# New order and engines for the second half of batch 0 and for batch 1 of a linear-attention and MLP-mixer kernel

## The chip, the cores and the metric

One core of a Trainium2 chip. The metric is the device time of the kernel in microseconds (us): the median of several executions. Inside the core five engines run their own instruction streams: PE (matrix products), DVE, ACT and POOL (element work), and SP (issues most of the transfers). POOL issues transfers too, on a queue of its own.

## The reference

Four batches, eight heads, 768 steps, 48 values per head and step. A linear attention with a decaying state is followed by a mixer of two perceptrons.

```python
for t in range(S):                       # S = 768
    kt, vt, rt = k[:, :, t], v[:, :, t], r[:, :, t]
    cur = einsum('bhd,bhe->bhde', u * kt, vt)
    y[:, :, t] = einsum('bhd,bhde->bhe', rt, state + cur)
    state = w * state + einsum('bhd,bhe->bhde', kt, vt)
x = y as (batch, 768, 384)
h = relu(xT @ w_tok1) @ w_tok2           # 768 -> 256 -> 768, over the steps
u = x + hT
out = u + relu(u @ w_ch1) @ w_ch2        # 384 -> 1536 -> 384, over the channels
```

## The kernel before

**Tiles.** A batch is cut into six chunks of 128 steps. `unit(b, c)` makes one chunk: scaled copies of k and r (`kr`), their transposes (`trk`, `tr_ps`, copied to `rka`, `rkb`), the scores (`at_ps`, masked to `AT`), the state (`kv_ps`, `S`), the chunk's outputs (`y_ps`) and the product of each step with itself, the own term (`ad_ps`, `adg`, then `ydb` or `yd`), all added to `x_b`. r of two chunks comes in one load, `win` (384 KB); k and v come chunk by chunk (`kt`, `vt`, 192 KB each). In batches 0 and 1 PE transposes; in batches 2 and 3 a transposing transfer does (`rk<-kr`, `uT<-u_sb`).

`mixer(b)` makes the rest of a batch: the hidden layer over the steps (`h_ps<-x_b,wtok`, `h1r`), back to the chunks and transposed (`hx_ps`, copied to `uT`, six pieces in two halves `sg` of three pieces `m`), the up products (`z_ps<-uT,wch`, 12 blocks `jt` for each half, relu to `zr`), the down products (`h_ps<-wch,zr`), the sum `osb` and its store.

**Order.** Each piece of work is a task with a number. A table written out by hand, `ORDER`, lists the numbers in the order in which they are emitted, and each engine keeps that order (`keep_in_program_order`), so that an instruction which waits holds everything behind it on its engine. `ENGINES` chooses the engine of every task that more than one engine can do, in the order in which these tasks are made; `BUFS` gives each tile its buffer. `FILL` puts products of zeros (`warm`) on PE ahead of a task. All are emitted through the same helper, so nearly every instruction has line 281 in the profile.

```python
    def run(self):
        done = set()
        for n in self.order:
            emit, deps = self.tasks[n]
            assert done.issuperset(deps), n
            self.now = n
            emit()
            done.add(n)
```

**Loads.** `load(b, c, i)` issues k, r or v (i = 0, 1, 2) on SP. `HOLD` lets a load of batch 0, and the first two of batch 1, wait until an earlier load has landed, so that four are in flight: r of (1,0) waits for v of (0,3), k of (1,0) for v of (0,4). `GATES` lets later loads wait for a weight: k of (1,2) for weight 2, v of (1,1) for weight 3. The seven weight transfers are issued by POOL between its other work: 0 `wtok1`, 1 `wtok2`, 2 the first four up blocks (`wch_0`), 3 the other eight (`wch_1`, 768 KB), 4 to 6 the thirds of the down weight; `W_DEP` lets some of them wait for a load.

```python
            if (b, c, i) in GATES:
                after(asked[b, c, i], sent[GATES[b, c, i]])
            if (b, c, i) in HOLD:
                after(asked[b, c, i], asked[HOLD[b, c, i]])
```

Of the kernel before, what the change touches and what calls it, by code (L numbers as in the profile page):

```python
# [60 lines left out]
]  # L61
BUFS = {
    'AT0': [
    0, 1, 2, 0, 1, 0, 2, 1, 0, 2, 0, 1, 0, 2, 1, 0, 2, 1, 0, 2, 1, 0, 2, 1,
],
    'AT1': [
    0, 1, 2, 0, 1, 0, 2, 1, 0, 2, 1, 0, 1, 2, 0, 2, 1, 0, 2, 0, 1, 2, 0, 1,
],
    'S0': [
    0, 1, 2, 0, 1, 2,  # L70
# [5 lines left out]
    0, 0, 0, 0,  # L76
],
    'adg': [
    0, 1, 2, 3, 4, 1, 2, 0, 3, 4, 1, 2, 0, 3, 4, 1, 2, 3, 1, 4, 3, 0, 2, 1,
],  # L80
    'h1r': [
    0, 1, 0, 1,
],
    'kp': [
    0, 1, 2, 3, 4, 5, 0, 1, 4, 2, 3, 0, 5, 1, 4, 2, 3, 5, 4, 0, 3, 1, 5, 2, 4, 3, 1, 0, 5, 2,
],
    'kt': [
    0, 1, 2, 3, 4, 5, 0, 1, 2, 3, 4, 5, 0, 1, 2, 3, 4, 0, 5, 1, 2, 3, 0, 4,
],
    'ku': [  # L90
    0, 1, 2, 0, 1, 0, 2, 0, 1, 2, 0, 2,
# [2 lines left out]
    0, 0, 0, 0, 0, 0, 0, 0, 0, 0,  # L94
],
# [8 lines left out]
],  # L104
    'osb': [
    0, 1, 2, 1, 0, 2, 2, 1, 0, 0, 2, 2, 2, 0, 1, 0, 0, 0, 2, 1, 0, 2, 1, 0, 2,
],
    'pr': [
    0, 1, 1, 0, 1, 0, 1, 0, 1, 0, 1, 0,
],  # L110
    'rk': [
    0, 1, 2, 3, 0, 1, 3, 2, 0, 1, 2, 3,
# [8 lines left out]
    0, 1, 0, 1, 0, 1, 1, 0, 0, 1, 0, 1,  # L121
],
    'rt': [
    0, 1, 2, 3, 4, 1, 2, 3, 0, 1, 4, 2,
],
    'uT': [
    0, 1, 2, 3, 0, 1, 2, 3,
# [2 lines left out]
    0, 1, 2, 3, 0,  # L130
],
    'vb': [
    0, 1, 2, 3, 4, 0, 1, 2, 3, 4, 0, 1, 2, 4, 0, 3, 1, 2, 4, 0, 1, 2, 3, 4,
],
    'vt': [
    0, 1, 2, 3, 4, 5, 0, 1, 2, 3, 4, 5, 0, 1, 2, 3, 5, 4, 0, 1, 2, 3, 5, 4,
],
    'win': [
    0, 1, 2, 1, 0, 2,
],  # L140
    'yd': [
    0, 1, 2, 0, 1, 2, 0, 1, 2, 0, 1, 2, 1, 0, 2, 1, 0, 1,
],
    'ydb': [
    0, 1, 0, 0, 1, 0,
],
    'zr': [
    0, 1, 2, 1, 0, 2, 1, 0,
],
}  # L150
ENGINES = [
# [25 lines left out]
WIDE_AT = [  # L177
    0, 1, 2, 3, 4, 5, 6, 7, 8, 9, 10, 11,
]
FILL = {138: 2, 154: 1, 159: 1, 190: 1, 160: 4, 907: 2}  # L180
POOL_ONLY = [
    2, 3,
]
# [59 lines left out]
def kernel(  # L243
# [63 lines left out]
    def fill(bank, fresh):  # L307
        for i in range(FILL.get(plan.now, 0)):
            pe.matmul(bank, warm[:, 0:128], warm[:, 0:bank.shape[-1]], start=fresh, stop=True, skip_group_check=True)
# [246 lines left out]
    def new_bank(tag):  # L556
        bank[0] = psum.tile([128, 512], f32, name="kv_ps", tag=tag, bufs=1)
# [630 lines left out]
    def keep_warm(cols):  # L1188
        def f():
            fresh = bank[0] is None  # L1190
            if fresh:
                new_bank("kv0")
            for i in range(1 + FILL.get(plan.now, 0)):
                pe.matmul(bank[0][:, 512 - cols:512], warm[:, 0:128], warm[:, 0:cols], start=fresh or cols == 512, stop=True,
# [40 lines left out]
```

## Time and profile before

| | |
|---|---|
| runs | 161.89, 162.02, 163.2 us (median 162.02) |
| profiled execution | 162.77 us, of which the span is 161.0 |
| PE busy | 153.7 us (95%) |
| DVE busy | 112.7 us (70%) |
| POOL busy | 88.0 us (55%) |
| ACT busy | 67.5 us (42%) |
| transferred | 26.88 MB, 167 GB/s on average |

The profile covers one execution. An engine is busy while it executes; PE's products are pipelined. A row of the timeline gives start, duration, engine, line and operation, with what is written and read, the shape, and how many are grouped; in brackets the idle time before the row and what ended it. A transfer is issued at its row's start and lands later. Transfers issued by SP run on queue q1, those by POOL on q0.

### The profile page before, as it was taken

The numbers are of one execution on the slowest core, as the hardware profiler recorded it, in microseconds if no ns is written. First come the engines' busy times: TensorE is split into PE (matmuls) and PEld (weight loads), VectorE is DVE, ScalarE is ACT, GpSimd is POOL, SyncE is SP. The second block draws the span as 40 slices with busy tenths as digits, with TensorE's granted clock in tenths as the row PEclk, the third lists the DMA queues.
The fourth block names the chain that finished last, engine by engine and source line by source line (L and its number), as shares of the span: only waits on it lengthen the run. The fifth ranks groups of instructions, "written<-read, shape, count | busy, mean of one in ns | idle before, by whom it ended". The sixth has DMA issues, their size and how long they took to land.

```text
span 161.0 us, 3787 instructions
## 1 busy us (share of the span) xinstructions
PE 153.7 (95%) x1464; PEld 102.3 (64%) x1465; DVE 112.7 (70%) x241; ACT 67.5 (42%) x151; POOL 88.0 (55%) x112
## 2 busy tenths in 40 slices
PE   6998889999999999999899999999999999999992
PEld 1455567767767776666577666677667556666672
DVE  6699889559648996586679946777999555616623
ACT  3998754735642551265357024256441101602100
POOL 7149675007437897999998997699724000000000
PEclk9999999999999999999999999999999999999999
DMA  4999999999999999997999999899991051701133
GB/s 123 221 210 190 147 240 199 145 204 187 212 218 199 175 199 180 253 175 174 183 236 191 203 227 180 162 236 226 140 234 70 0 122 49 219 4 49 49 139 106
DMA packets 93060, 26.88 MB, mean 167 GB/s; under 512 B 87794, under 2 KB 92148, under 8 KB 93044
## 3 DMA queue, kind: packets, MB, share of 16 engines
q1 hardware_dynamic: 90688, 23.40, 74.1%
q0 software_dynamic: 2160, 3.15, 11.7%
q8 instruction: 11, 0.18, 0.5%
q10 hardware_dynamic: 196, 0.11, 0.2%
q14 instruction: 5, 0.04, 0.1%
HBM read 20.46 MB, written 4.72 MB: 156 GB/s over the span
## 4 chain that ended last, share of the span: by engine, by line
PE 55%; DMA 20%; POOL 14%; DVE 4%; issue 3%; ACT 1%; SPq 1%; POOLq 0%; DVEq 0%; ACTq 0%
PE h_ps L281 23%; PE z_ps L281 19%; DMA kt<-in_k_dram 12%; POOL kr L281 8%; DMA rk<-kr 7%; PE y_ps L281 4%; POOL ku L281 3%; PE at_ps L281 3%; PE kv_ps L281 2%; POOL rku L281 2%; PE hx_ps L281 2%; DMA out_dram<-osb 2%; DVE AT L281 1%; POOL yd L281 1%; PE hT_ps L281 1%
## 5 line engine op out<-in xcount | busy, mean ns | idle before, releaser
L281 PE MATMUL h_ps<-wch,zr 128*128 128x384 bf16 (+1 forms) x300 | 54.3, 320 | 0.0
L281 PE MATMUL z_ps<-uT,wch 128*128 128x384 bf16 x288 | 51.8, 326 | 0.0
L281 ACT ACTIVATE zr<-z_ps 128x384 bf16<-128x384 f32 x62 | 28.4, 492 | 42.5 <-PE z_ps L281 42.3
L281 PEld LDWEIGHTS <-wch 128*128 128x128 bf16 x288 | 31.7, 114 | 13.1
L281 PEld LDWEIGHTS <-zr 128*128 128x128 bf16 x300 | 27.2, 98 | 15.4 <-issue 0.2
L281 DVE TENSOR_TENSOR AT<-at_ps,mask 128x512 bf16<-128x512 f32 x48 | 31.1, 684 | 6.5 <-PE at_ps L281 6.2
L281 POOL TENSOR_TENSOR kr<-kt,wnat 128x384 bf16<-128x384 f32 x21 | 20.9, 998 | 18.5 <-DMA kt<-in_k_dram 17.8
L281 DVE TENSOR_SCALAR zr<-z_ps 128x384 bf16<-128x384 f32 x34 | 18.5, 554 | 11.6 <-PE z_ps L281 11.4
L281 POOL TENSOR_TENSOR yd<-vb,adg 128x384 f32<-128x384 bf16 x18 | 14.9, 829 | 6.7 <-ACT vb L281 4.3
L281 PEld LDWEIGHTS <-kr 128*128 128x128 bf16 x176 | 11.2, 99 | 5.0 <-issue 1.0
L281 ACT CAST vb<-vt 128x384 bf16<-128x384 f32 x22 | 10.9, 513 | 8.2 <-DMA vt<-in_v_dram 8.0
L281 DVE TENSOR_TENSOR osb<-u_sb,h_ps 128x384 f32<-128x384 bf16 (+1 forms) x16 | 8.3, 526 | 7.3 <-PE h_ps L281 4.6
L281 POOL TENSOR_TENSOR rku<-ku,rt 128x384 f32<-128x384 f32 x12 | 11.9, 998 | 0.1
L281 POOL TENSOR_TENSOR kr<-rt,wp 128x384 bf16<-128x384 f32 x12 | 11.9, 999 | 0.1
L281 POOL TENSOR_TENSOR ku<-kt,u_bc 128x384 f32<-128x384 f32 x12 | 11.9, 999 | 0.0
L281 DVE TENSOR_TENSOR x_b<-y_ps,yd 128x384 bf16<-128x384 f32 x18 | 9.6, 551 | 1.9 <-PE y_ps L281 1.1
L281 PEld LDWEIGHTS <-wtok 128*128 128x128 bf16 x78 | 7.4, 98 | 4.4
L281 DVE TENSOR_TENSOR u_sb<-x_b,hT_ps 128x384 bf16<-128x384 bf16 x15 | 7.8, 550 | 2.9 <-PE hT_ps L281 2.7
L281 PE MATMUL h_ps<-x_b,wtok 128*128 128x384 bf16 x48 | 8.8, 326 | 0.0
L281 ACT ACTIVATE h1r<-h_ps 128x384 bf16<-128x384 f32 x4 | 2.0, 491 | 16.2 <-PE h_ps L281 16.2
L281 PE MATMUL y_ps<-vb,AT 128*128 128x48 bf16 x192 | 8.8, 183 | 0.0
L281 PEld LDWEIGHTS <-rk 64*128 64x128 bf16 (+1 forms) x136 | 5.3, 95 | 3.4 <-DMA rk<-kr 1.4
(96 smaller groups left out, 182.0 us busy)
## 6 DMA issues: line engine op xcount, KB each, us to landing
kt<-in_k_dram SPq DMA_DIRECT2D x24, 192.0 KB, 4.8
vt<-in_v_dram SPq DMA_DIRECT2D x24, 192.0 KB, 4.1
out_dram<-osb SPq DMA_DIRECT2D x23, 192.0 KB, 2.3
win<-in_r_dram SPq DMA_DIRECT2D x6, 384.0 KB, 6.0
rt<-in_r_dram SPq DMA_DIRECT2D x12, 192.0 KB, 4.1
wch<-in_moe_w_ch_dram POOLq DMA_DIRECT2D x4, 384.0 KB, 6.9
wtok<-in_moe_w_tok_dram POOLq DMA_DIRECT2D x2, 384.0 KB, 6.0
wch<-in_moe_w_ch_dram POOLq DMA_DIRECT2D x1, 768.0 KB, 8.9
```

Source lines behind the costliest of these rows:

```text
L281: return lambda *args, **kw: tc.keep_in_program_order(f(*args, **kw))
```

## The change

Only tables change: `ORDER`, `BUFS`, `ENGINES` and `FILL`. The tasks and what they compute stay. `ORDER` is new from the middle of batch 0 on to about the down products of batch 0's mixer and the last chunk of batch 1, and holds small swaps after that; from the hidden layer of batch 1's mixer on, PE's order is the old one. `HOLD`, `GATES` and `W_DEP` are the old ones. Five products of zeros go (one ahead of the scores of a chunk of batch 0, four ahead of an output), three come in ahead of the state of chunk 2.

```diff
 ORDER = [
...
-    906, 136, 156, 907, 185, 41, 152, 204, 66, 169, 131, 190, 205, 153, 141, 67, 50, 143, 170, 40, 191, 142, 171, 119,
+    906, 136, 156, 907, 185, 152, 66, 169, 131, 153, 174, 50, 67, 170, 137, 141, 176, 190, 142, 204, 40, 175, 69, 167,
...
-    222, 226, 209, 214, 223, 232, 227, 224, 219, 197, 228, 225, 216, 237, 217, 229, 122, 333, 230, 233, 231, 334, 246,
+    215, 209, 224, 228, 214, 196, 232, 227, 219, 122, 197, 225, 216, 229, 217, 333, 237, 230, 233, 231, 334, 240, 234,
...
 ENGINES = [
-    0, 0, 1, 0, 1, 1, 1, 1, 1, 0, 1, 0, 1, 1, 1, 0, 0, 0, 1, 0, 1, 1, 1, 1, 0, 1, 1, 0, 0, 0, 1, 1, 0, 0, 0, 0, 0, 0,
+    0, 0, 1, 0, 1, 1, 1, 1, 1, 0, 1, 0, 1, 1, 1, 0, 0, 1, 1, 0, 1, 1, 1, 1, 0, 1, 1, 0, 0, 0, 1, 1, 0, 1, 0, 0, 0, 0,
...
-FILL = {138: 2, 154: 1, 159: 1, 190: 1, 160: 4, 907: 2}
+FILL = {138: 2, 154: 1, 159: 1, 907: 2, 177: 3}
```

The first place is POOL at the end of batch 0, where it issues the weights: before the change its rows there are these. `ydb` are own terms, `kr_71<-kt` is the key product of the last chunk of batch 0, `wtok_100` and `wtok_101` are the token weights, `wch_0` and `wch_1` the two parts of the up weight; `kr_67<-kt` belongs to chunk 2 of batch 1.

```order
L281 TENSOR_TENSOR wGm_94<-bm,wG_91 128x384
L281 DMA wtok_100<-in_moe_w_tok_dram 128x6x256
L281 TENSOR_TENSOR ydb<-vb,adg 128x384 x2
L281 TENSOR_TENSOR kr_71<-kt,wnat_84 128x8x48
L281 DMA wtok_101<-in_moe_w_tok_dram 128x1536
L281 DMA wch_0_102<-in_moe_w_ch_dram 128x3x512
L281 TENSOR_TENSOR ydb<-vb,adg 128x384 x2
L281 DMA wch_1_103<-in_moe_w_ch_dram 128x3x1024
L281 TENSOR_TENSOR kr_67<-kt,wnat_84 128x8x48
```

And these are they after the change:

```order
L281 TENSOR_TENSOR wGm_94<-bm,wG_91 128x384
L281 DMA wtok_100<-in_moe_w_tok_dram 128x6x256
L281 TENSOR_TENSOR kr_71<-kt,wnat_84 128x8x48
L281 DMA wtok_101<-in_moe_w_tok_dram 128x1536
L281 DMA wch_0_102<-in_moe_w_ch_dram 128x3x512
L281 TENSOR_TENSOR ydb<-vb,adg 128x384 x2
L281 DMA wch_1_103<-in_moe_w_ch_dram 128x3x1024
L281 TENSOR_TENSOR kr_69<-win,wpair 128x8x48
L281 TENSOR_TENSOR kr_67<-kt,wnat_84 128x8x48
```

The two own terms ahead of the last key product are gone from that place (one is done earlier, one on DVE), and with it the second token weight and both parts of the up weight move up. A product of the first window of batch 1 has come over from DVE.

The second place is DVE at the start of batch 0's up products, before the change. `kr_70<-kt` is the key product of chunk 0 of batch 1, `uT` are the pieces that the up products read.

```order
L281 TENSOR_TENSOR kr_69<-win,wpair 128x8x48 x2
L281 TENSOR_SCALAR h1r<-h_ps 128x384
L281 CAST uT<-hx_ps 128x3x128
L281 TENSOR_TENSOR kr_70<-kt,wnat_84 128x8x48
L281 CAST uT<-hx_ps 128x3x128
L281 COPY rka<-trk 128x512
L281 TENSOR_SCALAR zr<-z_ps 128x384 x2
```

After the change DVE has there:

```order
L281 TENSOR_TENSOR kr_69<-win,wpair 128x8x48
L281 TENSOR_SCALAR h1r<-h_ps 128x384
L281 TENSOR_TENSOR kr_70<-kt,wnat_84 128x8x48
L281 CAST uT<-hx_ps 128x3x128 x5
L281 TENSOR_TENSOR AT_721<-at_ps,mask 128x512
L281 TENSOR_TENSOR AT_730<-at_ps,mask 128x512
```

Five of the six pieces of `uT` are now cast by DVE (two before), and all five stand behind the key product, of which one stood ahead before. On PE the transposes of that key product (`trk`) stand ahead of the last back product and of the up products, where before they stood behind all back products.

The third place is POOL in the up products, where the thirds of the down weight (`wch_104`) are issued, before the change:

```order
L281 TENSOR_TENSOR kr_67<-kt,wnat_84 128x8x48
L281 DMA wch_104<-in_moe_w_ch_dram 128x1536
L281 TENSOR_TENSOR kr_68<-kt,wnat_84 128x8x48
L281 DMA wch_104<-in_moe_w_ch_dram 128x1536 x2
L281 TENSOR_TENSOR kr_71<-kt,wnat_84 128x8x48
```

and after it:

```order
L281 TENSOR_TENSOR kr_67<-kt,wnat_84 128x8x48
L281 DMA wch_104<-in_moe_w_ch_dram 128x1536
L281 TENSOR_TENSOR kr_72<-kt,wnat_84 128x8x48
L281 DMA wch_104<-in_moe_w_ch_dram 128x1536
L281 TENSOR_TENSOR kr_68<-kt,wnat_84 128x8x48
L281 DMA wch_104<-in_moe_w_ch_dram 128x1536
```

The last third stands behind one more key product. On SP the window of chunks 4 and 5 of batch 1 is issued ahead of the keys of chunks 3 and 1, where it stood six loads later.

More of the change, by code (lines that the diff above doesn't have):

```diff
@@ L63 @@
     'AT0': [
-    0, 1, 2, 0, 1, 0, 2, 1, 0, 2, 0, 1, 0, 2, 1, 0, 2, 1, 0, 2, 1, 0, 2, 1,
+    0, 1, 2, 1, 0, 2, 1, 0, 2, 1, 2, 0, 1, 0, 2, 1, 0, 2, 1, 0, 2, 1, 0, 2,
 ],
     'AT1': [
-    0, 1, 2, 0, 1, 0, 2, 1, 0, 2, 1, 0, 1, 2, 0, 2, 1, 0, 2, 0, 1, 2, 0, 1,
+    0, 1, 2, 1, 0, 2, 1, 0, 2, 1, 0, 2, 1, 0, 2, 0, 1, 2, 0, 2, 1, 0, 2, 1,
 ],
@@ L78 @@
     'adg': [
-    0, 1, 2, 3, 4, 1, 2, 0, 3, 4, 1, 2, 0, 3, 4, 1, 2, 3, 1, 4, 3, 0, 2, 1,
+    0, 1, 2, 3, 4, 1, 0, 2, 3, 4, 1, 0, 2, 3, 4, 1, 0, 3, 1, 4, 3, 2, 0, 1,
 ],
@@ L84 @@
     'kp': [
-    0, 1, 2, 3, 4, 5, 0, 1, 4, 2, 3, 0, 5, 1, 4, 2, 3, 5, 4, 0, 3, 1, 5, 2, 4, 3, 1, 0, 5, 2,
+    0, 1, 2, 3, 4, 5, 0, 1, 4, 2, 3, 0, 4, 5, 1, 2, 4, 3, 2, 1, 0, 3, 5, 4, 2, 0, 3, 1, 5, 4,
 ],
     'kt': [
-    0, 1, 2, 3, 4, 5, 0, 1, 2, 3, 4, 5, 0, 1, 2, 3, 4, 0, 5, 1, 2, 3, 0, 4,
+    0, 1, 2, 3, 4, 5, 0, 1, 2, 3, 4, 5, 0, 1, 2, 3, 4, 5, 0, 1, 2, 3, 4, 5,
 ],
@@ L96 @@
     'm': [
[7 rows of a table removed]
[7 rows of a table added]
 ],
     'osb': [
-    0, 1, 2, 1, 0, 2, 2, 1, 0, 0, 2, 2, 2, 0, 1, 0, 0, 0, 2, 1, 0, 2, 1, 0, 2,
+    0, 1, 2, 2, 1, 0, 0, 2, 1, 1, 0, 0, 0, 1, 2, 1, 1, 1, 0, 2, 1, 0, 2, 1, 0,
 ],
     'pr': [
-    0, 1, 1, 0, 1, 0, 1, 0, 1, 0, 1, 0,
+    0, 1, 1, 0, 1, 0, 1, 0, 1, 1, 0, 1,
 ],
@@ L123 @@
     'rt': [
-    0, 1, 2, 3, 4, 1, 2, 3, 0, 1, 4, 2,
+    0, 1, 2, 3, 4, 2, 1, 3, 0, 2, 4, 1,
 ],
@@ L132 @@
     'vb': [
-    0, 1, 2, 3, 4, 0, 1, 2, 3, 4, 0, 1, 2, 4, 0, 3, 1, 2, 4, 0, 1, 2, 3, 4,
+    0, 1, 2, 3, 4, 1, 0, 2, 3, 4, 1, 0, 2, 4, 3, 1, 0, 2, 4, 3, 0, 2, 1, 4,
 ],
     'vt': [
-    0, 1, 2, 3, 4, 5, 0, 1, 2, 3, 4, 5, 0, 1, 2, 3, 5, 4, 0, 1, 2, 3, 5, 4,
+    0, 1, 2, 3, 4, 5, 0, 1, 2, 3, 4, 5, 0, 1, 2, 3, 4, 5, 0, 1, 2, 3, 4, 5,
 ],
@@ L141 @@
     'yd': [
-    0, 1, 2, 0, 1, 2, 0, 1, 2, 0, 1, 2, 1, 0, 2, 1, 0, 1,
+    0, 1, 2, 0, 1, 0, 2, 1, 0, 2, 1, 0, 1, 2, 0, 1, 2, 1,
 ],
     'ydb': [
-    0, 1, 0, 0, 1, 0,
+    0, 1, 0, 1, 0, 1,
 ],
```

86 rows, old and new, of tables (BUFS, ENGINES, ORDER) are left out of this document.

## The prediction

> **What bounds the kernel now.** I read the page first (busy shares and slices), then the busy time by stretch, then the timelines of POOL, DVE and PE around the end of batch 0, then the DMA view in short windows. All rows are of the kernel before; its profiled execution took 162.77 us, 161.0 of them span, so 1.77 us lie around the span, and it stands 0.75 above the median 162.02.
>
> ```profile
> PE 153.7 (95%) x1464; PEld 102.3 (64%) x1465; DVE 112.7 (70%) x241; ACT 67.5 (42%) x151; POOL 88.0 (55%) x112
> PE   6998889999999999999899999999999999999992
> DVE  6699889559648996586679946777999555616623
> POOL 7149675007437897999998997699724000000000
> ```
>
> TensorE is at 95%; the only slices (4 us each) below 9 after the start are those of 12 to 24 us and one near 78. DVE is full in the slices of 24 and of 52 to 60 us; POOL is full from 60 to 100. So time can be won only where PE is loose, and lost wherever something makes PE wait between 26 and 160 us. The stretches (PE, PEld, DVE, ACT, POOL busy) say how much:
>
> ```profile
> 14.00:18.00 4.00, 3.58 (x57) 2.38 (x60) 3.09 (x7) 3.35 (x9) 3.87 (x5) 1.00 1.41 189
> 18.00:22.00 4.00, 3.35 (x62) 2.29 (x63) 3.27 (x8) 2.62 (x6) 2.84 (x4) 1.00 1.07 149
> 22.00:26.00 4.00, 3.60 (x53) 2.39 (x49) 3.85 (x9) 2.20 (x6) 2.30 (x4) 1.00 1.21 250
> 26.00:31.00 5.00, 5.00 (x60) 3.77 (x58) 3.40 (x8) 3.03 (x6) 1.15 (x2) 1.00 1.04 157
> 55.00:63.00 8.00, 7.91 (x122) 5.78 (x120) 7.82 (x18) 3.25 (x9) 7.51 (x9) 1.00 1.17 200
> 78.58 0.62 PE L281 MATMUL at_ps<-rk 64*128 64x128 bf16 x16 [0.54 <-DMA rk<-kr]
> ```
>
> From 14 to 26 us PE idles 0.42 + 0.65 + 0.40 = 1.47 us; from 26 to 31 not at all. After that the slack is 0.09 us in 55 to 63, and the 0.54 us for which scores wait at 78.58 for a transposed product. The clock column (1.00) is full throughout.
>
> **The change part by part.** *The front, 14 to 31 us.* Zero products go: one of 512 columns and four of 384; three of 384 come in elsewhere.
>
> ```profile
> 15.39 0.38 PE L281 MATMUL at_ps<-warm 128*128 128x512 bf16 x1
> 18.24 0.82 PE L281 MATMUL y_ps<-warm 128*128 128x384 bf16 x4
> 16.89 1.02 POOL L281 DMA_DIRECT2D wtok<-in_moe_w_tok_dram  x1
> 19.16 1.61 POOL L281 TENSOR_TENSOR ydb<-vb,adg 128x384 bf16<-128x384 bf16 x2 [1.25 <-ACT vb L281]
> 20.74 0.99 POOL L281 TENSOR_TENSOR kr<-kt,wnat 128x384 bf16<-128x384 f32 x1
> 21.68 0.61 POOL L281 DMA_DIRECT2D wtok<-in_moe_w_tok_dram  x1
> 22.28 0.76 POOL L281 DMA_DIRECT2D wch<-in_moe_w_ch_dram  x1
> 26.34 0.81 POOL L281 DMA_DIRECT2D wch<-in_moe_w_ch_dram  x1
> ```
>
> Four products of 384 take 0.82 with the pipeline's tail, so 0.2 each at most: the net of -1 x 0.38 - 4 x 0.2 + 3 x 0.2 is -0.58 at most, and nothing at least, since the zeros stand where PE had no data. On POOL the last key product of batch 0 now stands ahead of the two own terms (1.61 us) behind which it ran at 20.74; its data let it start about 19.8, an estimate 0.97 us earlier. PE's gain by the first up product lies between nothing and 1.47 + 0.58 = 2.05; I take 1.3, since the two long waits in the stretch of 18 to 22 are for this chunk and its states.
>
> *The weights, issued from POOL.* With the product 0.97 earlier, the second token weight and the first up weight behind it are issued at about 20.8 and 21.4 instead of 21.68 and 22.28; the large up weight at about 21.4 + 0.76 + 1.61 = 23.8 instead of 26.34, if the two own terms ahead of it find their data. What do earlier weights do to the loads of batch 1, which SP issues on another queue?
>
> ```profile
> kt<-in_k_dram SPq DMA_DIRECT2D x1, 192.0 KB, 6.5
> q1 hardware_dynamic: 1848, 0.55, 112.6%
> q0 software_dynamic: 65, 0.03, 11.8%
> ...
> q0 software_dynamic: 24, 0.07, 84.1%
> q1 hardware_dynamic: 217, 0.04, 59.1%
> ...
> q0 software_dynamic: 83, 0.25, 94.6%
> q1 hardware_dynamic: 108, 0.02, 10.9%
> ...
> q0 software_dynamic: 235, 0.67, 96.2%
> q1 hardware_dynamic: 349, 0.07, 13.2%
> ...
> q0 software_dynamic: 168, 0.34, 107.4%
> wch<-in_moe_w_ch_dram POOLq DMA_DIRECT2D x1, 768.0 KB, 8.9
> ```
>
> These are windows of the DMA view: the load of keys of batch 1, chunk 0, issued at 19.09 (6.5 us to land, so 25.59); then the queues' packets in 22 to 24 us, 24 to 24.5, 39.5 to 41, 42.5 to 46, and 30 to 32 (q1 has no row there, so nothing moved, though loads were queued); last the large weight, issued at 26.34 (landed 35.26). q0 carries POOL's weights, q1 SP's loads. Almost alone, q1 moves 1848 packets in 2 us, 924 per us. Beside weights it gets 108 for 83, 349 for 235 and 0 for 168 weight packets, so 0 to 1.5 load packets for one weight packet. The window pair (r of chunks 0 and 1) and this key load are 1024 packets each, and in the kernel before nearly all of their 2048 pass in 22 to 24.5 us: in the gap between the first token weight's end and the second one's beginning. That second weight, issued at 21.68, had moved nothing by 24 (the 65 packets of 0.03 MB are 512 bytes each, the first weight's), so it needs 2.3 us to start; issued at 20.8 it starts at 23.1. By then at most 1.1 x 924 = 1,016 load packets are through, and some 1,030 are left against weight packets of 3 KB (384 KB: 128), 1 KB (384) and 2 KB (768 KB: 384), 896 in all without a pause. The weights' 1.57 MB at 0.25 MB in 1.5 us to 0.67 in 3.5, so 0.17 to 0.19 MB per us, last 8.3 to 9.2 us, to about 32.
>
> Upper bound: no load packet passes beside weights, and the keys land at 32 + 1030/924 = 33.1. In the middle, 1.4 load packets per weight packet: 735 weight packets are enough, 1.14 of the 1.57 MB, so 6.3 us, and with the loads' own 0.27 MB 1.5 more: 30.9. Lower bound: as in 24 to 24.5, 217 for 24, and the loads are through by 26, which costs nothing. I take 32.2, nearer to the rows from long windows (the half microsecond at 24 is the weight's first, in which its packets had reached only some of the 16 engines).
>
> The Trainium skill, "DMA: Bandwidth & Descriptors", section "Queues, rings and completion order", says that each DMA engine goes round-robin between its queue rows, draining a whole packet of some 9 to 17 descriptors before it switches. By that, if the trace's packets are those descriptors, the small loads would get several for each large weight descriptor and be hardly delayed; the window at 24 agrees (9 for one), the three longer ones do not (1.3, 1.5 and 0 for one).
>
> *What waits for these keys.*
>
> ```profile
> 29.27 0.56 DVE L281 CAST uT<-hx_ps 128x384 bf16<-128x384 f32 x1 [0.92 <-PE hx_ps L281]
> 29.74 0.55 DVE L281 TENSOR_TENSOR kr<-kt,wnat 128x384 bf16<-128x384 f32 x1
> 30.87 0.39 PE L281 MATMUL trk<-ident,kr 128*128 128x128 bf16 x4
> 31.09 3.09 PE L281 MATMUL z_ps<-uT,wch 128*128 128x384 bf16 x18
> 34.11 0.40 PE L281 MATMUL at_ps<-rkb,rka 64*128 64x128 bf16 x8
> ```
>
> Before, the product of the keys ran on DVE at 29.74, 4 us after they had landed. In the new order it stands on DVE ahead of five of the six casts of uT, and its transposes on PE ahead of the last back product and all ups. So a late load stops DVE, which casts nothing, and PE, whose ups need the casts. From the landing T: product 0.55, two casts at the spacing of 29.27 to 29.74, 0.47 each, then the ups of the half that they complete: first up at T + 1.5. Seven ups of 3 matmuls (18 in 3.02, 0.50 each) and one set of scores (0.40) precede the first up of the large weight, which starts at T + 5.4. In the old order the same work from 31.09 would reach it at 31.09 + 3.5 + 0.4 = 35.0. So this stage ends T - 29.6 later: +2.6 at T = 32.2, +3.5 at 33.1, +1.3 at 30.9. The front's 1.3 is swallowed by the wait and is not to be subtracted.
>
> *The ups' weight.* Issued 2.5 us earlier, it still runs behind the other weights on its queue. It landed at 35.26, just before its first up. At most the pause between weights is saved: landing about 34.4, a bound for any gain of 0.6 at this point.
>
> *Behind it, 35 to 63 us.* Same products in a new mix. On POOL the two last thirds of the down weight are issued with key products between them, so the last is some 2 us later than here:
>
> ```profile
> 39.41 1.14 POOL L281 DMA_DIRECT2D wch<-in_moe_w_ch_dram  x2
> L281 POOL TENSOR_TENSOR kr<-kt,wnat 128x384 bf16<-128x384 f32 x21 | 20.9, 998 | 18.5 <-DMA kt<-in_k_dram 17.8
> ```
>
> POOL waited 17.8 us in all for key loads, so each product that is put ahead of a weight can hold it. Against that, POOL has three tasks fewer; DVE, full at 7.82 of 8 in 55 to 63, gets more than it gives. From nothing to +1; with the keys late already, PE is behind and these weights have the time: I take 0. Of the +2.6, a lag at 35 us is made up where PE waits for others: 0.09 in 55 to 63 and 0.54 at 78.58, together 0.6; from nothing to all of it.
>
> *Sum:* 0 (front, swallowed) + 2.6 - 0.6 = +2.0. On the profiled execution's 162.77 that is 164.8; on the median 162.02, **164.0 us**. Its own range: T of 30.9 to 33.1 with and without the 0.6, 162.7 to 165.6, and up to 166 if held loads behind it land late too.
>
> **The rivals.** *The loads get through (faster).* If q1 shares as at 24 to 24.5, T stays below 29 and PE has its 1.3 at the first up. The ups of the large weight may then cost the most of it, but POOL has three tasks fewer (0.8 each, half of the 1.61), so its chain, full from 60 to 100, can start up to 2.4 earlier: 162.02 - 2.4 = 159.6. For it speaks the window at 24 (217 for 24), against it the three longer ones. By the Trainium skill's rule on queue rows, above, this would be the outcome. *The gain is eaten (no change).* Keys in time, but the large weight lands at 34.4 and the last of the down weights lands later; of 1.3 remain 0.3: 161.7. For it: PE's 5.00 of 5 after 26 us, so no slack is left to win; against it: POOL's shorter list. A wait for the last down weight belongs here too: both of these weights were issued within 39.41 and 40.55, and 2 us later with 6.5 to 8 us to land is 49 to 51.
>
> ```profile
> 50.99 0.81 PE L281 MATMUL h_ps<-wch,zr 128*128 128x384 bf16 x4
> ```
>
> The products of this stage that need it run around 51, so it costs +1 at most, 163.0, and decides only if it lands after 51.6. That the zero products do it is no rival: 0.58 us at most, where PE waits anyhow.
>
> **How the numbers follow.** A measurement of this kernel tells about 1% (1.6 us) from no change: faster is below 160.4, slower above 163.6. Late keys: 0.52, of which 0.48 over 1% and 0.04 within. The loads get through: 0.24, of which 0.23 over 1% faster and 0.01 within. Eaten, or the last weight's wait: 0.24, of which 0.17 within, 0.01 faster and 0.06 slower. So faster 0.24, same 0.22, slower 0.54. The range reaches from just under the faster rival to the upper bound: 159.5 to 166.2.
>
> **What would show it.** Right: the keys of batch 1, chunk 0 land at 30.9 or later, DVE idles before its product `kr<-kt,wnat` with DMA as releaser, PE has a wait of over 1.5 us ahead of the ups (`trk` or `hx_ps`, traced back to that load), and the first up of the large weight starts at 36.3 to 38.5. In the windows after 23 us q0 is over 90% and q1 gets fewer than two packets per weight packet. Wrong: the keys land before 29 and the ups start before 31; then whether POOL's full stretch after 60 us starts earlier decides between the two other cases. It would be wrong in size if the lag of the ups is more than made up by 63 us, or if the transposes of batch 2 wait longer at 78 us than 0.54.

## The result, and the profile after

The changed kernel takes 161.44 us (median of 22 executions, 160.85 to 164.66) where the kernel before takes 162.38 in the same comparison: ratio 0.9944, 95% interval 0.9923 to 0.9965. It is about 0.6% faster, not slower. The forecast was 164.0 with a chance of 0.54 for slower by over 1%; its range of 159.5 to 166.2 holds the time only because it reaches down to the faster rival; the direction was wrong.

The profiled execution took 161.94 us, its span 160.2. First the parts of the page that answer to those of before:

```profile
span 160.2 us, 3792 instructions
PE 152.1 (95%) x1463; PEld 101.4 (63%) x1463; DVE 113.5 (71%) x244; ACT 67.6 (42%) x152; POOL 85.0 (53%) x109
PE   6888889999999999999999999999999999999990
DVE  6689996668895994687779945877999544525721
POOL 7048595033932589999998995999542000000000
```

PE is as full as before, the loose slice near 78 us is gone. Then POOL, DVE and PE around the end of batch 0, the issue row of the keys of batch 1, chunk 0 (issued at 19.27), and the queues' packets in 22 to 24, 24 to 24.5 and 24.5 to 26 us:

```profile
20.05 0.99 POOL L281 TENSOR_TENSOR kr<-kt,wnat 128x384 bf16<-128x384 f32 x1 [1.74 <-DMA kt<-in_k_dram]
20.99 0.61 POOL L281 DMA_DIRECT2D wtok<-in_moe_w_tok_dram  x1
23.93 0.81 POOL L281 DMA_DIRECT2D wch<-in_moe_w_ch_dram  x1
27.25 0.55 DVE L281 TENSOR_TENSOR kr<-kt,wnat 128x384 bf16<-128x384 f32 x1
29.49 2.42 DVE L281 CAST uT<-hx_ps 128x384 bf16<-128x384 f32 x5 [1.70 <-PE hx_ps L281]
28.32 1.78 PE L281 MATMUL hx_ps<-wtok,h1r 128*128 128x384 bf16 x10 [0.27 <-DMA wtok<-in_moe_w_tok_dram]
30.66 0.65 PE L281 MATMUL z_ps<-uT,wch 128*128 128x384 bf16 x3
...
kt<-in_k_dram SPq DMA_DIRECT2D x1, 192.0 KB, 7.2
...
q1 hardware_dynamic: 1308, 0.44, 85.3%
q0 software_dynamic: 223, 0.11, 39.9%
...
q1 hardware_dynamic: 581, 0.11, 116.3%
q0 software_dynamic: 7, 0.02, 21.6%
...
q0 software_dynamic: 99, 0.30, 101.3%
q1 hardware_dynamic: 190, 0.04, 15.5%
```

The weights were issued when the prediction said (20.99, 23.93). But the 223 weight packets of 22 to 24 us are 512 bytes each, all of the first weight: the second one had moved nothing by 24. The loads (q1) passed in between, as before: when the second weight moved its first packet, at 24.14, some 570 of the 2,048 load packets were left. In the half microsecond from 24 on 581 load packets passed beside 7 of the weight, and in the 1.5 us behind it the last 190 beside 99. The keys landed at 26.5, and their product on DVE ran at 27.25 without a wait. The ups started at 30.66, 0.43 earlier than before, and nothing waited for the keys.

### The profile page after: what moved, and what is told of

Its sections match the earlier page's. It is cut to its first block, busy times and chain, and to the rows that moved or that the text cites. A ratio compares the mean times of both kernels' runs of the same rounds, so it can differ in the third digit from the quotient of the medians.

```text
span 160.2 us, 3792 instructions
## 1 busy us (share of the span) xinstructions
PE 152.1 (95%) x1463; PEld 101.4 (63%) x1463; DVE 113.5 (71%) x244; ACT 67.6 (42%) x152; POOL 85.0 (53%) x109
## 3 DMA queue, kind: packets, MB, share of 16 engines
q0 software_dynamic: 2160, 3.15, 11.3%
## 4 chain that ended last, share of the span: by engine, by line
PE 77%; DMA 16%; DVE 2%; ACT 1%; issue 1%; POOL 1%; SPq 0%; ACTq 0%; POOLq 0%
PE h_ps L281 33%; PE z_ps L281 29%; DMA vt<-in_v_dram 6%; DMA wtok<-in_moe_w_tok_dram 5%; PE y_ps L281 4%; PE hT_ps L281 3%; DMA kt<-in_k_dram 3%; DMA win<-in_r_dram 3%; PE at_ps L281 3%; PE hx_ps L281 2%; PE kv_ps L281 1%; PE trk L281 1%; ACT rkb L281 1%; POOL kr L281 1%; PE tr_ps L281 1%
## 5 line engine op out<-in xcount | busy, mean ns | idle before, releaser
L281 POOL TENSOR_TENSOR kr<-kt,wnat 128x384 bf16<-128x384 f32 x20 | 19.9, 999 | 19.8 <-DMA kt<-in_k_dram 19.6
L281 ACT CAST vb<-vt 128x384 bf16<-128x384 f32 x24 | 12.1, 512 | 10.9 <-DMA vt<-in_v_dram 10.9
L281 PE MATMUL kv_ps<-warm 128*128 128x512 bf16 (+1 forms) x17 | 5.9, 490 | 1.9 <-DVE warm L281 1.3
```

Source lines behind the costliest of these rows:

```text
L281: return lambda *args, **kw: tc.keep_in_program_order(f(*args, **kw))
```

## The experiments

All changes are to tables, two lines of code in the runs on the tail aside; medians are those of the comparison, ratios are to the kernel before.

**Both weights early (w_early).** The price of the mechanism that the prediction bet on, with the gap between the weights taken away.

```diff
 ORDER, of the change
-    ... 119, 157, ... 180, 120, 188, ... 221, 121, 203, ...
+    ... 119, 120, 121, 157, ... 180, 188, ... 221, 203, ...
```

> The changed kernel with the second token weight and the first up weight issued on POOL right behind the first token weight (about 18.3 us instead of 21.0 and 21.6). Theory S, that of the prediction: a weight's packets begin some 2.3 us after its issue, so here they follow the first weight's without a gap at about 22.8, and the keys of batch 1, chunk 0 get through only beside weights: they land at 30 to 33 us (changed kernel: 26.5), the ups start at 32 to 34.5 (30.7), and the time is 1.5 to 3 us above the changed kernel, 163 to 164.5. Theory G: on these rings the second weight does not begin before some 1.4 us after the first weight's last packet, whenever it is issued, and the loads pass in that gap: keys at 26 to 27, ups at 30.5 to 31, time within 0.5 of the changed kernel.

Measured: 167.97 us, ratio 1.0346 (1.0299 to 1.0394). The profile, first the queues in 20 to 22 and 22 to 24 us and the two loads' issue rows (issued at 17.95 and 19.12), then who waits, and PE's busy time in 26 to 31 and 31 to 35.5 us:

```profile
q0 software_dynamic: 669, 0.34, 127.3%
q1 hardware_dynamic: 156, 0.03, 12.0%
...
q0 software_dynamic: 192, 0.39, 103.8%
q1 hardware_dynamic: 82, 0.03, 9.4%
...
win<-in_r_dram SPq DMA_DIRECT2D x1, 384.0 KB, 11.5
kt<-in_k_dram SPq DMA_DIRECT2D x1, 192.0 KB, 14.9
29.42 0.56 DVE L281 TENSOR_TENSOR kr<-win,wpair 128x384 bf16<-128x384 f32 x1 [4.26 <-DMA win<-in_r_dram]
34.07 0.56 DVE L281 TENSOR_TENSOR kr<-kt,wnat 128x384 bf16<-128x384 f32 x1 [3.62 <-DMA kt<-in_k_dram]
PE tr_ps L281 <- POOL kr L281: 3.9, 1, 3.9
26.00:31.00 5.00, 1.10 (x13) 0.73 (x11) 1.03 (x2) 0.68 (x2) 1.35 (x1) 0.92 1.17 230
31.00:35.50 4.50, 4.46 (x33) 3.03 (x32) 1.43 (x4) 1.82 (x3) 0.58 (x1) 0.71 1.05 223
35.71 0.49 PE L281 MATMUL z_ps<-uT,wch 128*128 128x384 bf16 x2 [0.25 <-DVE uT L281]
```

Theory S holds here in its mechanism: with 861 weight packets in 20 to 24 us the loads move 238, the window lands at 29.4, the keys at 34.0, and the ups start at 35.71, 1.6 after the keys' product, where the prediction had 1.5. Its numbers were too small: the keys were expected at 30 to 33, the ups at 32 to 34.5, and by the two ratios the time is 6.5 us above the changed kernel, not 1.5 to 3. The window is late too, which the prediction did not reckon with: the 3.9 us for which PE stands (1.10 busy of 5 in the row of 26 to 31) are a wait for the window's product on POOL. The clock column falls to 0.92 and 0.71 around this wait; in the kernel before it is 1.00 throughout. Theory G falls: a weight does follow the one ahead without a gap if it is issued early enough. The Trainium skill's page "DMA: Bandwidth & Descriptors" (section "Queues, rings and completion order") has each DMA engine go round-robin between queue rows, a whole packet at a time; the prediction took from it that the loads could get several packets for each of a weight's. These two windows show 0.2 and 0.4 load packets for one weight packet, but 28 to 30 us of the same run has 402 for 177, so no run here gives one ratio.

**Both weights late (w_late).**

```diff
 ORDER, of the change
-    ... 180, 120, 188, ... 221, 121, 203, ... 219, 122, ...
+    ... 180, 188, ... 221, 203, ... 219, 120, 121, 122, ...
```

> The changed kernel with the second token weight and the first up weight issued behind the two own terms, at about 22.7 and 23.3 us. Theory S: keys of batch 1, chunk 0 land at 25.5 to 26 (26.5 in the changed kernel), the second token weight at about 29 (28.3), so the back products on PE start at 29.1 instead of 28.3 and the time rises by 0.5 to 0.8 us. Theory G: the weight still starts at about 24.2 to 24.9, the keys land as in the changed kernel, and the time is 0 to 0.6 us above it.

Measured: 163.51 us, ratio 1.0051 (1.0015 to 1.0088). The second weight was issued at 23.86 (the own term waited for its data); its first packet came 1.3 us later, at 25.18. So the start is not a fixed 2.3 us behind the issue: 1.3 with the loads through, 3.15 in the changed kernel (20.99 to 24.14) with the loads running, 2.24 before (21.68 to 23.92). By the two ratios it costs 1.7 us against the changed kernel, more than the 0.5 to 0.8 of Theory S or the 0 to 0.6 of Theory G. The back products, which Theory S made late, start at 28.40, as in the changed kernel (28.32); the loss lies behind them and was not traced further.

**The second token weight at 19.3 and at 20.0 us (w_1930, w_2005).** Where does the harm begin?

```diff
 ORDER, of the change: 120 ahead of 218
-W_DEP = [(0, 2, 2), None, (0, 4, 2), (0, 1, 0), (0, 5, 2), None, (0, 1, 0)]
+W_DEP = [(0, 2, 2), (0, 4, 2), (0, 4, 2), (0, 1, 0), (0, 5, 2), None, (0, 1, 0)]   # w_1930
+W_DEP = [(0, 2, 2), (0, 5, 0), (0, 4, 2), (0, 1, 0), (0, 5, 2), None, (0, 1, 0)]   # w_2005
```

> The changed kernel with the second token weight alone issued earlier, ahead of the last key product of batch 0 and made to wait for the landing of v of chunk 4, so at about 19.3 us (21.0 in the changed kernel, 18.1 in the run with both weights early). Theory A (first come): the side whose transfers reach the engines first goes first. The first window of batch 1 is issued at 18.2 and its keys at 19.3, so here the weight comes between them: window landed by 26, keys not before 28, ups 0.5 to 3 us later than in the changed kernel (30.7) and the time 1 to 3 us above it. Theory B (fixed sharing, as in the prediction): the weight follows the first one at 22.5 without a gap, window and keys both pass only beside weights, keys at 30 or later, 3 us or more above the changed kernel.

> As before, but waiting for the landing of the last keys of batch 0, so issued at about 20.0 us, 1 us earlier than in the changed kernel; the key product behind it on POOL comes 0.6 us later. Theory A (first come): window and keys of batch 1, issued at 18.2 and 19.3, are ahead of it; keys land by 27, and the time is within 0.6 us of the changed kernel (the later product alone costs up to 0.6). Theory B (sharing decides from the weight's start, 2.3 us after its issue): it starts at 22.6, the keys land at 29 or later, 2 us or more above the changed kernel.

Measured: two times each. w_1930: 162.46, 162.76, 168.67, 168.68. w_2005: four executions of 162.49 to 163.38, five of 168.80 to 169.99 (a tenth, at 310, was disturbed). No theory said that there would be two. The profile of w_1930 is of a lower time; the window (issued at 17.26), the keys (19.47), then who waits:

```profile
win<-in_r_dram SPq DMA_DIRECT2D x1, 384.0 KB, 7.4
kt<-in_k_dram SPq DMA_DIRECT2D x1, 192.0 KB, 10.3
29.74 0.56 DVE L281 TENSOR_TENSOR kr<-kt,wnat 128x384 bf16<-128x384 f32 x1 [2.17 <-DMA kt<-in_k_dram]
31.38 0.65 PE L281 MATMUL z_ps<-uT,wch 128*128 128x384 bf16 x3 [0.30 <-ACT rka L281]
```

The weight, issued at 19.71, moves its first packet at 23.30, 0.5 us behind the first weight's last. The window lands at 24.7, the keys only at 29.7, DVE waits 2.17 us for them, and the ups start at 31.38. That is the course of Theory A, and the wait that the prediction was about, at a small price: some 0.7 to 1 us above the changed kernel. The upper times fit Theory B and are near that of w_early, but no trace of them was taken; that it is the same wait is an inference. What decides between the two is open, and so is whether the changed kernel is quite clear of it: one of its 12 executions in the comparison with its second profile took 170.57 us. In w_2005 the lower times (ratio 1.0021) are about 1 us above the changed kernel, more than the 0.6 of Theory A.

**Front and rest apart (front_a, front_b).**

```diff
 ORDER, ENGINES, FILL, cut at task 279, the first up product
+    front_a: of the change up to the cut, of before from there on
+    front_b: of before up to the cut, of the change from there on
```

> Order, engines and zero products of the changed kernel up to the first up product of batch 0, of the kernel before from there on; buffers dealt anew. If the gain of the changed kernel comes from the front (first up product 0.43 us earlier in its profile), the hidden layer of batch 1 starts 0.4 us earlier than before or more (62.6 or less, before 62.98), the wait of 0.54 us at 78.6 for a transposed product stays, and the time is 0.3 to 0.5 us below the kernel before. If it comes from the part behind the ups alone, the 0.43 are lost by 63 us (large up weight, down weights) and the time is that of before within 0.2.

> The other half: order, engines and zero products of the kernel before up to the first up product, of the changed kernel from there on; buffers dealt anew. If the part behind the ups brings its own gain (0.33 us between the first up product and the hidden layer of batch 1, and 0.61 us at 78 us, where the wait for the transposed product is gone because POOL has three tasks fewer), the hidden layer starts at about 62.6 and the time is 0.7 to 1.0 us below before, whatever the front does. If these need the early front, the time is that of before within 0.3.

Measured: front_a 161.96 us, ratio 0.9954 (0.9918 to 0.9989); front_b 162.24, ratio 0.9994 (0.9968 to 1.002). By the times the front brings a gain and the rest alone brings none. Not all went as expected: in front_a the first up product starts at 30.41, 0.7 to 0.85 earlier than in the two profiles of before (31.09 and, below, 31.26), but the hidden layer of batch 1 at 62.87, only 0.1 to 0.3 earlier, and the wait at 78 us is not there. In front_b the only wait of PE that the profile lists between 26 and 64 us is one for a copy of transposed keys (`rka`):

```profile
32.27 0.40 PE L281 MATMUL at_ps<-rkb,rka 64*128 64x128 bf16 x8 [0.35 <-ACT rka L281]
```

The scores of batch 1 stand earlier in the new order, and with the old front that copy is not ready. The large weight, issued as late as before, does not hold PE in this profile.

**The same two kernels again (before2, after2).** For a second profile of each.

> The kernel before once more, for a second profile. If the wait of 0.54 us at 78.6 for the transposed product, and the time from the last product to the span's end (2.95 us), are the kernel's own, they are seen again within 0.15 us; if they differ from one execution to the next, the hidden layer of batch 2 follows that of batch 1 after 29.2 to 29.5 us (29.93 in the first profile).

> The changed kernel once more: time 0.4 to 0.8% below before. In its second profile PE again reaches the up products 0.3 to 0.6 us and the hidden layer of batch 1 0.6 to 0.9 us earlier than the kernel before; the 3.75 us from the last product to the span's end fall to about 3 if they were this execution's own.

Measured: before2 0.9992 (0.9965 to 1.0019), after2 0.9958 (0.9921 to 0.9994). The second profile of the changed kernel reaches the ups 1.4 and the hidden layer of batch 1 1.7 us earlier than that of before, more than expected. Profiled executions: 162.1 and 161.26 us. PE from 26 to 31 and from 70 to 110 us, first before2, then after2, with the scores that waited 0.54 us in the first profile of before:

```profile
26.00:31.00 5.00, 5.00 (x58) 3.81 (x57) 3.40 (x8) 2.86 (x6) 1.31 (x2) 1.00 1.11 180
70.00:110.00 40.00, 40.00 (x383) 27.19 (x382) 29.41 (x58) 18.16 (x44) 36.91 (x41) 1.00 1.05 201
78.13 0.62 PE L281 MATMUL at_ps<-rk 64*128 64x128 bf16 x16
...
26.00:31.00 5.00, 5.00 (x56) 3.46 (x55) 3.68 (x8) 2.65 (x5) 0.00 (x0) 1.00 1.17 211
70.00:110.00 40.00, 40.00 (x389) 27.23 (x388) 29.54 (x58) 17.49 (x41) 37.15 (x41) 1.00 1.09 206
29.86 0.65 PE L281 MATMUL z_ps<-uT,wch 128*128 128x384 bf16 x3
```

The wait at 78 us was that one execution's: PE is at 40.00 of 40 in both. Starts on PE, in us (the profiles' zero differs by up to 0.2):

| | before | before2 | after | after2 |
|---|---|---|---|---|
| last hidden product, batch 0 | 27.43 | 27.59 | 26.25 | 26.24 |
| first up product, batch 0 | 31.09 | 31.26 | 30.66 | 29.86 |
| hidden layer, batch 1 | 62.98 | 63.13 | 62.21 | 61.40 |
| last product | 157.80 | 157.13 | 156.21 | 155.43 |
| end of the span | 161.0 | 160.4 | 160.2 | 159.6 |

PE's last product comes 1.6 to 1.7 us earlier, the end only 0.8. The difference lies behind PE: 3.2 and 3.3 us there before, 4.0 and 4.1 after the change. The expectation that the long tail was one execution's own fell.

**The tail (a_act3, b_act3).** Last store issue of before2 and the queues in 2 us behind it (from 0.25 us after that issue); the same of after2:

```profile
157.80 0.33 SPq L281 DMA_DIRECT2D out_dram<-osb  x1
q1 hardware_dynamic: 241, 0.22, 31.7%
q10 hardware_dynamic: 144, 0.10, 15.4%
span 160.4 us, 3788 instructions
...
156.09 0.33 SPq L281 DMA_DIRECT2D out_dram<-osb  x1
q1 hardware_dynamic: 240, 0.22, 32.3%
q10 hardware_dynamic: 144, 0.10, 15.3%
q14 instruction: 1, 0.01, 1.2%
span 159.6 us, 3792 instructions
```

The span ends 2.6 us after the last store's issue there and 3.5 here, and one packet on the instruction queue q14 lies in between. Both kernels got three more small ACT instructions, at 117 us (the two expectations count from a product 0.25 us ahead of the last one, so their tails are 0.25 longer than those above):

```diff
         def copy_v(on):
             L["vb"] = sb("vb", [128, dm], bf16)
             copy(on, L["vb"], loaded[b, c, 2])
+            if plan.now in (749, 770, 778):
+                copy(on, L["vb"][:, 0:48], loaded[b, c, 2][:, 0:48])
```

> The changed kernel with three more instructions on ACT, copies of 48 of the 384 columns that the casts of v of chunks 3 to 5 of batch 3 have just written (about 117 us, where ACT is mostly idle); nothing else changes. In the profiles of the changed kernel one packet of 8 KB on the instruction queue (q14) moves 2.0 to 2.3 us after the start of the last product, and the last store's packets end at 2.9 to 3.0 us after it; in those of the kernel before q14 moves at 4.0 and the store ends at 2.2. Theory F: it is ACT's instruction fetch, at a fixed place of its stream (ACT has 195 recorded instructions against 192), and it delays the last store. With three more the fetch falls 10 us or more earlier, the span ends 3.5 us after the start of the last product (4.25 and 4.38 in the two profiles of the changed kernel), and the time is 0.6 to 0.9 us below the changed kernel, about 1.0% below before. Theory T: the tail comes from something else (buffers, the order of stores); it stays at 4.2 to 4.4 and the time at that of the changed kernel.

> The kernel before with the same three instructions on ACT (195 recorded ones, as the changed kernel has). Theory F: the fetch now falls into the last store, the span ends 4.1 to 4.4 us after the start of the last product (3.49 and 3.51 before), and the time is 0.6 to 0.9 us (0.4 to 0.55%) above before. Theory T: tail 3.5, time that of before within 0.2 us.

Measured: a_act3 160.80 us, ratio 0.9915 (0.9882 to 0.9949); b_act3 163.17, ratio 1.0053 (1.0027 to 1.0079). a_act3, then b_act3:

```profile
157.19 0.33 SPq L281 DMA_DIRECT2D out_dram<-osb  x1
span 159.8 us, 3795 instructions
...
158.43 0.33 SPq L281 DMA_DIRECT2D out_dram<-osb  x1
q14 instruction: 1, 0.01, 2.2%
span 161.9 us, 3791 instructions
```

Theory F holds both ways: three instructions take the packet out of the changed kernel's last store (2.6 us from its issue to the end) and put it into that of the kernel before (3.5). That the instructions were ACT's alone shows whose fetch it is. The other runs agree. With 191 or 192 ACT instructions recorded the packet comes behind the end of the span (five profiles). With 195 it comes during the last store, and the tail is 3.8 to 4.1 us (six profiles). With 197 (front_a) and 198 (a_act3) it comes at 145.8 and 140.3 us, and the tail is 3.2.

a_act3 is faster than both kernels. Its profile shows that the front's gain is not the same in every execution: the first token weight landed late, and the last hidden product starts at 27.37, hardly earlier than before. (This execution took 161.47 us; the median of the run is 160.80.)

```profile
24.70 1.15 PE L281 MATMUL h_ps<-x_b,wtok 128*128 128x384 bf16 x6 [0.95 <-DMA wtok<-in_moe_w_tok_dram]
```

**Parts of the front (b_pool, b_nofill).**

```diff
 b_pool: ORDER of before, 137 ahead of 40, 218 behind 119; ENGINES: 173 on DVE
 b_nofill: of before
-FILL = {138: 2, 154: 1, 159: 1, 190: 1, 160: 4, 907: 2}
+FILL = {138: 2, 154: 1, 159: 1, 907: 2, 177: 3}
```

> The kernel before with POOL's order at the end of batch 0 alone as in the changed kernel: one own term ahead of the first token weight, the other on DVE, the last key product right behind that weight, so that it starts at 20.0 instead of 20.9 and the two weights behind it are issued at 21.0 and 21.6. If the front's gain is that key product's 0.9 us, the last hidden product starts 0.7 to 1.0 us earlier than before and the time is 0.5 to 0.8 us below before. If it needs the new order on PE, DVE and ACT around it, hidden products and time move by less than 0.3 us.

> The kernel before with the zero products of the changed kernel (five gone, three new), nothing else. If they fill time in which PE waits for data, PE's later products start within 0.15 us of before, and the time is that of before within 0.2 us; if they hold up work, 0.4 to 0.6 us are won.

Measured: b_pool 163.19, ratio 1.0044 (1.0016 to 1.0071); b_nofill 162.53, ratio 1.0012 (0.999 to 1.0034). Neither is the gain. In b_pool the last hidden product starts at 27.21, 0.2 to 0.4 earlier, and the hidden layer of batch 1 at 64.06, 0.9 to 1.1 later; 0.89 of it is one wait among the ups, for `zr` from DVE. Its buffers were dealt anew, as in front_a and front_b, so POOL's order does not stand alone in it. In b_nofill the last hidden product starts at 27.98, 0.4 to 0.55 later than before, not within 0.15; the time is that of before within the interval. So taking the zero products out wins nothing, as the prediction had it; that they filled nothing but idle time is not shown.

## Why the prediction was wrong

**The step that failed** is the landing time T of the keys: 32.2 in the sum, 26.5 measured. Two terms of it were wrong.

The first is "issued at 20.8 it starts at 23.1". The issue was right (20.99); the start was 24.14, 23.91 and 24.40 in three profiles with this order. The 2.3 us were read from one case in which the loads were running, and taken for the weight's own; with nothing else moving it took 1.3 (w_late), with the first weight's last packets and the loads ahead of it up to 3.4. Which of these two held it was not tested apart. So some 570 load packets were left when the weight began, not 1,030.

The second is "0 to 1.5 load packets for one weight packet" from the weight's first packet on. In the changed kernel 581 load packets passed beside 7 in the first half microsecond, as in the row of 24 to 24.5 before (217 for 24), which the prediction set aside. w_1930 shows this term by itself: there the weight did start at 23.30, with some 1,000 load packets left, and the keys still landed at 29.7, below the prediction's middle of 30.9. By its own rule (T - 29.6) that costs 0.1 us. The row of "0 for 168" in 30 to 32 us is a weak one: its loads were issued only at 29.75 and 30.16, and in the changed kernel a load issued at 29.95, also beside the large weight, moves nothing until 31.60, so the row may show their start and not their share. (The middle has a slip too: 735 packets of these sizes are 1.24 MB, not 1.14, which makes it about 31.5.)

With T at 26.5 the term of +2.6, and with it the +2.0, falls to nothing.

**What was right.** The chain behind late keys: from their product to the first up it took 1.6 us in w_early (34.07 to 35.71) and in w_1930 (29.74 to 31.38), forecast 1.5 from the landing. By the sum's rule the stage of w_early ends 34.07 - 29.6 = 4.5 later; the first up does by 4.6 (before 31.09). That taking out the zero products wins nothing was right too. The front's 1.3 at the first up product lies between the 0.43 and 1.40 of the two pairs of profiles; one execution (a_act3) had 0.1 to 0.3. The rival in which the loads get through was the one that came about in its cause, and not by its amount: 2.4 us less than before by its sum, 0.3 by that of "the gain is eaten", 0.9 measured. Its 2.4 were to come from POOL, whose first product of r of batch 2 (`kr<-rt,wp`) starts at 61.74 and 60.92 after the change, 62.26 and 62.33 before: 0.5 to 1.4 earlier.

**Where the gain went.** Of 1.2 us at the last hidden product 0.43 were left at the first up in the first profile. The second token weight landed later than before (28.3, before 27.7), and the back products waited 0.27 for it; POOL's product of the window, 1.36 us long, held its transposes by 0.20. In the second profile PE did not idle there and 1.4 were left. The large weight, issued at 23.93 and 9.8 us under way, landed at 33.7, and PE did not wait for it. At the last product PE is 1.6 and 1.7 us earlier in the two pairs. Then the instruction fetch took 0.75 to 0.9, which no row of the profile before could show, as it fell behind the last store there.

The two halves add to this unequally. From the first up to the last product PE takes 125.5 to 125.6 us in the two profiles of the changed kernel and in a_act3, 125.9 and 126.7 before, 126.4 in front_a. So, by these profiles, the rest does bring something once the front is new. front_a lacks that part, and its last product starts at 156.77, 0.6 to 1.3 later than in the changed kernel; but it lacks the long tail too, 0.75 to 0.9 of it. That is why its time equals that of the changed kernel within the intervals, and why a_act3, which has both halves and the short tail, is at 0.9915.

**The 0.6 us of slack** that the sum took off rested mostly on a wait of one execution (0.54 at 78.58); the second profile of before has no such wait.

**What stays open.** What decides in w_1930 and w_2005 between the two times; and which of the front's moves on PE, DVE and ACT bring its gain, since POOL's order and the zero products alone do not.

## What to carry to other kernels

A transfer's start, read from one trace, holds what was ahead of it: before it is used as a latency for another order, look for a case where nothing else was moving. Where two queues share the engines, the price of a collision and its chance are two questions; a range that follows from the price alone is too sure of the sign. And read the last microseconds too: a gain on the busiest engine counts only if the span's end moves with it.

## What the runs showed of the hardware

- Which of two queues gets the DMA engines depends on what is running: beside running weights the loads got 238 packets for 861 in 20 to 24 us (w_early); while loads were running, a weight that had just begun got 7 packets beside 581 in 24 to 24.5 (changed kernel). No share held throughout: in 24 to 29 of w_1930 it was 467 load packets for 616.
- From issue to its first packet the same weight took 1.3 us with the loads through (w_late) and 2.9 to 3.4 with the first weight and loads running (changed kernel, three profiles).
- With this weight's issue at 19.3 to 20.0 us the same program has two times 6 us apart (w_1930: 162.5 and 168.7); the cause of the upper one is not traced.
- One 8 KB packet on the instruction queue during the last store comes with a tail of 3.8 to 4.1 us from PE's last product to the end, against 3.2 to 3.3 without; where it falls goes with the number of ACT instructions (behind the end with 191 and 192 recorded ones, in the store with 195, 11 us or more ahead of it with 197 and 198).
